# Linear attention and an affine MLP on one core: one k-v layout for batches 2 to 7, the bias column in batch 1, g on VectorE, and a re-planned order

## The chip, the cores and the metric

The kernel runs on one core of one Trainium2 chip, in one launch. The core has five engines that matter here: TensorE (PE in the profile), VectorE (DVE), ScalarE (ACT), GpSimd (POOL), and SyncE (SP), which here only issues transfers. Each engine takes its own instructions strictly in order and waits on semaphores for the others. The metric is device time in microseconds, the median of several runs.

## The reference

The inputs are q, k and v of shape [8 batches, 8 heads, 576 rows, 64], and the parameters of a residual MLP with affine scales in place of a norm. All is float32.

```python
kv  = einsum('bhsd,bhse->bhde', k, v)            # 64 x 64 for each head
out = einsum('bhsd,bhde->bhse', q, kv)
x   = out / sqrt(mean(out**2, -1) + 1e-6) * g_norm   # heads side by side: [8, 576, 512]
a1  = alpha1 * x + beta1
tok = einsum('ts,bsd->btd', w_tok, a1)           # w_tok: 576 x 576
u   = x + lam * tok
a2  = alpha2 * u + beta2
out = u + lam * (relu(a2 @ w_ch1) @ w_ch2)       # 512 -> 2048 -> 512
```

## The kernel before

The kernel does not issue instructions as it is read. `Prog.op` records every operation with its engine (or a choice of engines), a cost in microseconds, what it reads and writes, and a priority. `plan` then derives urgencies from a few operations with due times, schedules all operations several times in a model (`schedule`), shuffles a few priorities (`shake`, with the seeds given to `plan`), and keeps the order. The instructions of each engine are emitted in that order, with semaphore waits where a result crosses engines. While the first channel matmul has not started, the model fills TensorE's idle time with warming matmuls on zeros (L1429 in the profile), so the number of these is a planned figure, fixed when the kernel is built.

For each of the eight batches the work is:

1. *Loads.* k, v and q of a batch come by SP. For batch 0, a row of the tile holds nine consecutive tokens of one head (`nine`). For batches 1 to 7 (`load_kv`) it holds four consecutive ones of the first 512 (`kf`, `vf`), and the 64 tokens from 512 on stand in tiles of their own (`kft`, `vft`), by two more loads each.
2. *The k-v product* (float32). Batch 0: `kv_first`, L628, two groups of 36 matmuls that contract over 64 rows. Batches 1 to 7: `kv_groups`, two groups of 16 matmuls over 128 rows (L691) and one of 8 over the 64 rows of the tails (L701). The result is split into a high and a low bfloat16 part (`kvd`) by ScalarE (L718) and VectorE (L723, L726).
3. *The q-kv product and the norm* (`qkv_groups`). q is split the same way (L501, L582) and transposed, for batches 0 and 1 by TensorE, later by transfers. The products are L789 for batch 0 (float32), L782 with L401 for the others, and `tail` (L863) for the last 64 tokens. Then come a square on ScalarE (L819), a sum over each head on VectorE (L821), a square root and a reciprocal, and x without g (L840). Two multiplications follow: by alpha1, lam and g into the bfloat16 operand of the token mix (`rt`, `rtt`; L844, L892), and by g into x itself, on GpSimd (L848, L895).
4. *The token mix* (`tok_groups`, L920 and L942; batch 0: `tok_first`, L972). It contracts over 576 tokens in five passes. The last pass holds the 64 tail tokens and one row with beta1 times lam, against which `wt` has a row with the sums of w_tok's rows. For even batches the tail tokens stand in partitions 0 to 63 and the beta1 row in 64, for odd ones in 64 to 127 and 0, so that `wt` keeps the tail rows and the sums twice (chunks 4 and 5). VectorE adds the result to x (L927).
5. *a2, transposed* (`a2t`). Batches 0 and 1: transposed on TensorE (`ut_pe`, L1007), with alpha2 and beta2 applied as the columns are evacuated (L1016, L1017). Later batches: only alpha2 is applied (L933), and a transfer transposes. Their beta2 enters as a bias of the ReLU (`hb`), beta2 times w_ch1.
6. *The channel matmuls.* `ch1_groups`: 16 tiles of 128 hidden columns (L1056 for even batches; L1075 for odd ones, which take the tail tokens of two batches along). In batch 0, each of its 64 matmuls is followed by one of a single column that multiplies beta2 by the same weights (L401 on `b2c`); these 16 columns become `hb`. Then `ch2_groups` (L1121; L1102 at the very end).

TensorE interleaves the end of one batch with the start of the next: the second channel matmul of a batch hides the token mix's evacuation, the k-v product of the next batch but one and the transpositions.

The weights are loaded on the same SP queue behind the first k, v and q, in the order w_tok, batch 1, w_ch1 in four parts, lam, w_ch2 in four parts. w_ch1 is converted to bfloat16 by ScalarE and VectorE (L501, L502), w_ch2 is multiplied by lam by VectorE and GpSimd (L1357).

Of the kernel before, what the change touches and what calls it, by code (L numbers as in the profile page):

```python
# [15 lines left out]
NH = 8  # L16
S = 576
# [32 lines left out]
class Prog:  # L50
# [6 lines left out]
    def __init__(self, nc, stack):  # L57
# [9 lines left out]
        self.spare = 0.0  # L67

# [54 lines left out]
    def plan(self, due, rounds, seeds):  # L123
# [40 lines left out]
        def shake(pri, seed):  # L164
            rnd = random.Random(seed)
            return {o: pri[o] + (rnd.gauss(0.0, 2.0) if rnd.random() < 0.1 else 0.0)
                    for o in movable}
# [12 lines left out]
    def schedule(self):  # L180
# [67 lines left out]

        while left:
            progressed = False  # L250
            for e, q in queues.items():
                while q and free[e] <= t + 1e-9:
# [3 lines left out]
                    for o in cands:  # L256
# [4 lines left out]
                        if isinstance(o.eng, tuple) and better_elsewhere(o, e, t):  # L261
                            continue
# [144 lines left out]
def bass_transnormer_attn__then__resmlp_affine_kernel(  # L407
# [15 lines left out]
    with ExitStack() as stack:  # L423
# [14 lines left out]
        b2c = sb("b2c", [128, 4], BF16)  # L438
        hb = sb("hb", [128, 16], F32)
        eps = sb("eps", [128, 1], F32)  # L440
        kf = sb("kf", [128, 2, NH, 4, DH], F32)
        vf = sb("vf", [128, 2, NH, 4, DH], F32)
        qf = sb("qf", [128, NH, 4, DH], F32)
        kft = sb("kft", [128, 2, 4, DH], F32)
        vft = sb("vft", [128, 2, 4, DH], F32)
# [18 lines left out]
        a2t = sb("a2t", [128, 4, TP], BF16)  # L464
# [9 lines left out]
        def nine(tile, a):  # L474
            return tile[:, a].rearrange("p h c d -> p (h c d)")[:, 0:1152].rearrange(
                "p (x c d) -> p x c d", x=2, c=9)

# [38 lines left out]

        HALVES = (slice(0, 4), slice(4, 8))
        ALL = (slice(0, 8),)

        def load_first(a):  # L520
            for key, src, tile in (("kf", k, kf), ("vf", v, vf)):
                P.op("SP", 0.6, lambda e, src=src, tile=tile: e.dma_start(
                    nine(tile, a).rearrange("p x c d -> p x (c d)"),
# [11 lines left out]
        def load_kv(b, go=()):  # L535
            j = (b + 1) % 2
            for tile, tl, src, n in ((kf, kft, k, "kf"), (vf, vft, v, "vf")):
                P.op("SP", 0.6, lambda e, tile=tile, src=src: e.dma_start(
                    tile[:, j].rearrange("p h c d -> p h (c d)"),
                    src[b, :, 0:512, :].rearrange("h (p c) d -> p h (c d)", c=4)),  # L540
                    r=go, w=[(n, j)], dma_us=3.4)
                for g in range(2):
                    P.op("SP", 0.5, lambda e, tl=tl, src=src, g=g: e.dma_start(
                        tl[64 * g:64 * g + 64, j],
                        src[b, 4 * g:4 * g + 4, 512:576, :].rearrange("h s d -> s h d")),
                        w=[(n + "t", j, g)], dma_us=0.4)
# [71 lines left out]

        def kv_first():

            def group(a):
                t = P.ptile(2)

                def f(e):
                    for c in range(9):
                        for x, y in ((0, 0), (0, 1), (1, 0), (1, 1)):
                            r = slice(64 * y, 64 * y + 64)
                            m = e.matmul(t.ap(slice(64 * x, 64 * x + 64))[:, y, 0:64],  # L628
# [833 lines left out]
```

## Time and profile before

| | |
|---|---|
| median of 3 runs | 368.38 us (367.87 to 368.93) |
| the profiled execution | 368.05 us, of which the span is 366.2 us |
| TensorE busy | 360.6 us, 98% |
| VectorE busy | 198.4 us, 54% |
| ScalarE busy | 159.2 us, 43% |
| GpSimd busy | 81.7 us, 22% |
| moved | 59.87 MB in 92423 packets, 163 GB/s on the mean |

The lines of the profile read: line of the kernel, engine, operation, output and inputs, shape, count, then busy time, mean duration in ns, and the engine's idle time ahead of it with what ended it. In rows in order of time the first two numbers are the start and the length of a group of alike instructions in microseconds, from the first one's start to the last one's end. A matmul's listed length includes its way through the array and overlaps the next one's, so the distance between starts is what it takes of TensorE's time. A float32 matmul that isn't a transposition appears as two records: "x72" of L628 is 36 matmuls.

### The profile page before, as it was taken

To read this page: it belongs to the slowest core of one execution; us is meant where nothing else is said; L and a number is where in the kernel's file an instruction comes from. 1 tells how busy PE (TensorE), PEld (TensorE's weight loads), DVE (VectorE), ACT (ScalarE), POOL (GpSimd) and SP (SyncE) were. 2 spreads that over 40 slices of the span, in tenths; PEclk is the share of its full clock that TensorE was granted. 3 is DMA by queue.
4 is the path that set the end of the run, shared out by engine and by line. 5 is a ranking of instruction groups with operands and counts; after the bars stand their busy time and mean duration, and the time that the engine had idled before them with its cause. 6 is when DMAs were issued, how large, how long until landed. Compare 5 with 4: busy or idle time off the path is not lost.

```text
span 366.2 us, 7069 instructions
## 1 busy us (share of the span) xinstructions
PE 360.6 (98%) x3164; PEld 205.8 (56%) x2876; DVE 198.4 (54%) x313; ACT 159.2 (43%) x268; POOL 81.7 (22%) x71
## 2 busy tenths in 40 slices
PE   7999999999999999999999999999999999999996
PEld 3787445467754554457654554457654554457644
DVE  4287699773973197735764176915933165720021
ACT  2464974237830298107650188107630186007600
POOL 4064602700450007100530006400620006200000
PEclk9999999999999999999999999999999999999999
DMA  8999999999777897439904499233404110420012
GB/s 257 319 290 319 384 382 273 265 250 249 211 141 158 246 259 178 101 94 309 230 18 115 138 304 177 50 110 85 90 7 108 59 30 0 59 100 30 0 57 88
DMA packets 92423, 59.87 MB, mean 163 GB/s; under 512 B 59549, under 2 KB 82341, under 8 KB 92264
## 3 DMA queue, kind: packets, MB, share of 16 engines
q1 hardware_dynamic: 92368, 59.41, 62.5%
q8 instruction: 24, 0.39, 0.5%
q14 instruction: 7, 0.06, 0.0%
q10 hardware_dynamic: 24, 0.01, 0.0%
HBM read 38.56 MB, written 9.44 MB: 131 GB/s over the span
## 4 chain that ended last, share of the span: by engine, by line
PE 97%; DMA 2%; SPq 0%; DVE 0%; issue 0%
PE ps L1121 34%; PE ps L1075 19%; PE ps L1056 16%; PE ps L920 8%; PE ps L691 4%; DMA qf<-in_q_dram 2%; PE ps L401 2%; PE ps L782 2%; PE ps L789 1%; PE ps L942 1%; PE ps L972 1%; PE ps L1007 1%; PE ps L1429 1%; PE ps L649 1%; PE ps L1102 1%; PE ps L701 1%
## 5 line engine op out<-in xcount | busy, mean ns | idle before, releaser
L1121 PE MATMUL ps<-w,ht 128*128 128x512 bf16 x560 | 126.0, 379 | 0.0
L848 POOL TENSOR_TENSOR xm<-xm,g_bc 128x512 f32<-128x512 f32 (+1 forms) x36 | 47.4, 1316 | 186.6 <-DVE rt L844 184.7
L1121 PEld LDWEIGHTS ps<-w,ht 128*128 128x128 bf16 x560 | 53.1, 98 | 63.0 <-issue 1.2
L1045 ACT ACTIVATE ht<-ps,hb 128x512 bf16<-128x512 f32 (+1 forms) x96 | 70.5, 739 | 40.5 <-PE ps L1075 32.8
L1075 PE MATMUL ps<-a2t,w 128*128 128x320 bf16 x512 | 71.9, 299 | 0.0
L1075 PEld LDWEIGHTS ps<-a2t,w 128*128 128x128 bf16 x512 | 49.3, 98 | 20.2 <-ACT ht L1045 0.3
L1056 PE MATMUL ps<-a2t,w 128*128 128x512 bf16 x256 | 59.7, 379 | 0.0
L1131 DVE TENSOR_TENSOR xm<-ps,xm 128x512 f32<-128x512 f32 x31 | 21.4, 689 | 50.4 <-PE ps L1121 50.3
L718 ACT ACTIVATE kvd<-ps 64x128 bf16<-64x128 f32 x28 | 7.6, 271 | 78.5 <-PE ps L701 78.1
L1056 PEld LDWEIGHTS ps<-a2t,w 128*128 128x128 bf16 x256 | 24.3, 97 | 29.6 <-issue 1.2
L821 DVE TENSOR_REDUCE small<-sq 128x16 f32<-128x1024 f32 (+2 forms) x20 | 20.5, 1028 | 22.9 <-ACT sq L819 22.9
L920 PE MATMUL ps<-rt,wt 128*128 128x512 bf16 x112 | 28.8, 379 | 0.0
L501 ACT ACTIVATE qs<-qf 128x1024 bf16<-128x1024 f32 (+1 forms) x15 | 14.2, 964 | 26.7 <-DMA qf<-in_q_dram 26.1
L927 DVE TENSOR_TENSOR xm<-ps,xm 128x1024 f32<-128x1024 f32 x14 | 17.1, 1222 | 14.5 <-PE ps L920 14.5
L1046 ACT ACTIVATE ht<-ps 128x512 bf16<-128x512 f32 (+1 forms) x32 | 20.6, 650 | 6.8 <-PE ps L1075 3.3
L819 ACT ACTIVATE sq<-ps 128x1024 f32<-128x1024 f32 (+2 forms) x20 | 17.4, 873 | 7.3 <-PE ps L789 4.3
L840 DVE TENSOR_TENSOR xm<-ps,small 128x1024 f32<-128x1024 f32 (+1 forms) x18 | 19.8, 1103 | 0.4
L723 DVE TENSOR_TENSOR kvd<-ps,kvd 64x128 bf16<-64x128 f32 x28 | 8.1, 288 | 20.5 <-ACT kvd L718 20.0
L844 DVE TENSOR_TENSOR rt<-xm,e1g_bc 128x1024 bf16<-128x1024 f32 (+1 forms) x17 | 19.0, 1125 | 0.1
L582 DVE TENSOR_TENSOR qs<-qf,qs 128x1024 bf16<-128x1024 f32 x12 | 15.3, 1284 | 6.8 <-ACT qs L501 6.8
L920 PEld LDWEIGHTS ps<-rt,wt 128*128 128x128 bf16 x112 | 10.9, 98 | 12.9 <-issue 0.4
L691 PEld LDWEIGHTS ps<-vf,kf 128*64 128x64 f32 x448 | 14.2, 138 | 5.0 <-issue 5.0
(119 smaller groups left out, 334.2 us busy)
## 6 DMA issues: line engine op xcount, KB each, us to landing
out_dram<-xm SPq DMA_DIRECT2D x31, 256.0 KB, 2.5
kf<-in_k_dram SPq DMA_DIRECT2D x7, 1024.0 KB, 10.3
vf<-in_v_dram SPq DMA_DIRECT2D x7, 1024.0 KB, 8.0
qf<-in_q_dram SPq DMA_DIRECT2D x7, 1024.0 KB, 8.0
stg<-in_moe_w_ch_dram SPq DMA_DIRECT2D x3, 1024.0 KB, 13.8
kf<-in_moe_w_ch_dram SPq DMA_DIRECT2D x2, 1024.0 KB, 14.6
kf<-in_k_dram SPq DMA_DIRECT2D x2, 576.0 KB, 5.2
vf<-in_v_dram SPq DMA_DIRECT2D x2, 576.0 KB, 6.3
```

Source lines behind the costliest of these rows:

```text
L691: m = e.matmul(out(h), kf[:, buf, h, c, :], vf[:, buf, h, c, :], start=(c == 0 and h < 4 * a + 2), stop=False, skip_group_check=True)
L821: P.op("DVE", dve_us(64 * m), lambda e: e.tensor_reduce(out=smv, in_=sqv.rearrange("p (h d) -> p h d", h=m), axis=AX.X, op=ALU.add), r=[(" ...
L840: P.op("DVE", dve_us(64 * m), lambda e: e.tensor_tensor(out=x3, in0=split(raw()), in1=inv, op=ALU.mult), r=[t, ("sm", sms)], w=xk, pri=-200)
L844: lambda e: e.tensor_tensor(out=r_, in0=x, in1=eb, op=ALU.mult),
L848: P.op("POOL", pool_us(64 * nh), lambda e, xc=xc: e.tensor_tensor(out=xc, in0=xc, in1=g_bc[rows, None, :].to_broadcast([nr, nh, DH]), op=A ...
L920: m = e.matmul(t.ap()[:, i, :], tok_w(b, sc, c), rsrc(b, sc), start=(sc == 0), stop=(sc == 4))
L1045: o = P.op("ACT", act_us(n) + 0.09, lambda e: e.activation(dst, src(), ACT.Relu, bias=hb[:, fj:fj + 1]) if b > 1 else e.activation(dst, sr ...
L1046: dst, src(), ACT.Relu, bias=hb[:, fj:fj + 1]) if b > 1 else e.activation(
L1056: m = e.matmul(t.flat(), w, a2t[:, dj, 0:512], start=(dj == 0), stop=(dj == 3))
L1075: m = e.matmul(t.ap()[:, i, 0:320], w1[:, dj, 128 * fj:128 * fj + 128], a2t[:, dj, 320 * i:320 * i + 320], start=(dj == 0), stop=(dj == 3))
L1121: m = e.matmul(t.flat(), ht[:, fj, 128 * c:128 * c + 128], w2[:, fj, :], start=(fj == 0), stop=(fj == 15))
L1131: P.op("DVE", dve_us(512), lambda e: e.tensor_tensor(out=x, in0=t.flat(), in1=x, op=ALU.add), r=[t] + keys, w=keys)
```

## The change

- k and v of batches 2 to 7 are loaded in batch 0's layout, nine tokens to a row, by one load each. `kv_product` serves batch 0 and, through `kv_nine`, these; the new evacuation does for each of the two groups what was done behind the third. Batch 1 keeps its form, with its tails in the free end of the same tile.
- The beta2 column moves from batch 0 to batch 1: `a2t` gets a column 640 with beta2, and in `odd` the second half of each tile takes 321 columns instead of 320. Sixteen copies of one column (`hb[:, fj]`) replace one of sixteen.
- Batch 0's first four tiles of the first channel matmul are computed in two halves, `front` and `back`, over two of the four contracted chunks each.
- From batch 2 on, VectorE multiplies x by g, over the pair of row blocks at once.
- The tail rows of the mix's operand always stand in partitions 0 to 63 with the beta1 row at 64. The second copy in `wt` and its sums are no longer made. Another form of the mix is added behind `MIX = 8`, which no batch reaches; two operations that only that form needs stay (a copy of `wt`'s tail rows, and beta1 loaded once more and multiplied by lam).
- The planner: a rule `sooner` (ScalarE, VectorE and GpSimd don't start a less urgent operation if a more urgent one becomes ready within half its cost), a different `shake` and seed, costs changed for batch 0's q-kv product and two evacuations, and parameter rows loaded in the order of the list.

The order of the instructions of every engine changes with it. The core of the diff:

```diff
+            share, by = (0.02, 0.1, 0.3)[seed % 3], (1.0, 3.0)[seed % 2]
+            return {o: pri[o] + (rnd.gauss(0.0, by) if rnd.random() < share else 0.0)
...
+        def sooner(o, e, t):
+            cost = o.cost[e] if isinstance(o.cost, dict) else o.cost
+            until = t + self.look * cost
...
+                    if t + 1e-9 < at <= until:
+                        return True
+            return False
...
+                        if e in ("ACT", "DVE", "POOL") and sooner(o, e, t):
+                            continue
...
-        def load_kv(b, go=()):
+        def load_kv(b):
             j = (b + 1) % 2
+                if b > 1:
+                    P.op("SP", 0.6, lambda e, src=src, tile=tile: e.dma_start(
+                        tile[:, j].rearrange("p (z f) -> p z f", z=4),
+                        src[b].rearrange("(z y) (p c) d -> (y p) z (c d)", y=2, c=9)),
+                        w=[(n, j)], dma_us=3.1)
+                    continue
...
+        def kv_product(b, a):
+            j = a if b == 0 else (b + 1) % 2
+            t = P.ptile(2)
+            def f(e):
+                for c in range(9):
+                    for x, y in ((0, 0), (0, 1), (1, 0), (1, 1)):
+                        r = slice(64 * y, 64 * y + 64)
+                        m = e.matmul(t.ap(slice(64 * x, 64 * x + 64))[:, y, 0:64],
+                                     nine(kf, b, a)[r, x, c, :], nine(vf, b, a)[r, x, c, :],
+                                     start=(c == 0), stop=(c == 8), skip_group_check=True)
+                return m
+            P.op("PE", 1.22, f, r=[("kf", j), ("vf", j)], w=[t])
+            return t
...
+        def kv_nine(b):
+            kv5 = kvd[:].rearrange("p (a x y) i d -> p a x y i d", a=2, x=2)
+            def group(a):
+                t = kv_product(b, a)
+                for x in range(2):
...
         def kv_groups(b):
+            if b > 1:
+                yield from kv_nine(b)
+                return
...
-                    P.op("PE", 0.28 * nc_, f32, r=QT + KVD + [("kv32", h0 // 4, i)
+                    P.op("PE", 0.55 * nc_ + 0.02, f32, r=QT + KVD + [("kv32", h0 // 4, i)
...
-                    P.op("POOL", pool_us(64 * nh), lambda e, xc=xc: e.tensor_tensor(
-                        out=xc, in0=xc, in1=g_bc[rows, None, :].to_broadcast([nr, nh, DH]),
+                    P.op("POOL" if b < 2 else "DVE", pool_us(n) if b < 2 else dve_sb(n),
+                         lambda e, xc=xc, gb=gb: e.tensor_tensor(
+                             out=xc, in0=xc, in1=gb, op=ALU.mult),
...
-                        if b == 0:
-                            m = P.matmul_held(hbt.flat()[:, fj:fj + 1], w, b2c[:, dj:dj + 1],
-                                              dj == 0, dj == 3)
...
+            def front(fj):
+                held[fj] = t = P.ptile(1)
+                def f(e):
+                    for dj in range(2):
+                        m = e.matmul(t.flat(), w1[:, dj, 128 * fj:128 * fj + 128],
+                                     a2t[:, dj, 0:512], start=(dj == 0), stop=False)
...
+                            n = 321 if (b, i) == (1, 1) else 320
...
+                if b == 1:
+                    P.op(act_dve(1), 0, lambda e: copy(
+                        e, hb[:, fj:fj + 1], t.ap()[:, 1, 320:321]), r=[t], w=[("hb", fj)])
...
-        spread_load(moe_alpha2, a2_bc, "a2")
+        spread_load(moe_alpha2, a2_bc[:], "a2")
+        spread_load(moe_beta1, stg[:, 0, 0, :], "st0")
         P.chain = False
+        P.op("DVE", dve_sb(512), lambda e: e.tensor_tensor(
+            out=lam_bc[:], in0=stg[:, 0, 0, :], in1=lam_bc[:], op=ALU.mult),
+            r=["st0"], w=["lam", "e2"], port=True)
+        P.op("DVE", 0.4, lambda e: e.tensor_copy(out=wt[64:128, 5, :], in_=wt[0:64, 4, :]),
+             r=[("wtm", 4)], w=["wt5"], port=True)
...
-        P.plan(due, 8, (15,))
+        P.plan(due, 8, (56,))
```

More of the change, by code (lines that the diff above doesn't have):

```diff
@@ L700, in f @@
                         rows = slice(64 * (h // 4), 64 * (h // 4) + 64)
-                        m = e.matmul(out(h), kft[rows, buf, h % 4, :], vft[rows, buf, h % 4, :],
+                        m = e.matmul(out(h), rows64(kf)[rows, h % 4, :], rows64(vf)[rows, h % 4, :],
                                      start=False, stop=True, skip_group_check=True)
                     return m
-                P.op("PE", 0.4, f, r=[(n + "ft", buf, g) for n in "kv" for g in range(2)], w=ts)
+                P.op("PE", 0.4, f, r=[(n + "ft", g) for n in "kv" for g in range(2)], w=ts)
                 for a in range(2):
```

255 lines of the change are left out of this document (166 added, 89 removed).

## The prediction

> **What bounds the kernel now.** I read the page's busy shares and the granted clock first, then the chain of work that ended last, then the order of time on TensorE.
>
> ```profile
> span 366.2 us, 7069 instructions
> PE 360.6 (98%) x3164; PEld 205.8 (56%) x2876; DVE 198.4 (54%) x313; ACT 159.2 (43%) x268; POOL 81.7 (22%) x71
> PEclk9999999999999999999999999999999999999999
> PE 97%; DMA 2%; SPq 0%; DVE 0%; issue 0%
> ```
>
> TensorE is 97% of the chain and its clock is full, so the time is the sum of what stands on TensorE's queue. But not all of that is work: warming matmuls fill planned waits.
>
> ```profile
> L1429 PE MATMUL ps<-a2b 128*128 128x512 bf16 x32 | 9.3, 437 | 1.9 <-DVE a2b L1226 1.9
> ```
>
> So a gain has two sources: real work taken off TensorE, or, in the stage before the first channel matmul, a wait (warming) that gets shorter. Everything on the other engines is free as long as its result is there when TensorE's fixed order reaches it. What a matmul costs is the distance from its start to the next one's, since its listed duration overlaps the next.
>
> **The change, part by part.** The new constant for the mixing form is 8 and the batches are 0 to 7, so its branches never run: the mix stays in five full passes for each of four row blocks.
>
> *The bias column.* Batch 0 loses its 64 one-column matmuls (four behind each of 16 tiles). Their price, in order of time, with the price of the same matmul without them from the chain:
>
> ```profile
> 38.72 0.38 PE L1056 MATMUL ps<-a2t,w 128*128 128x512 bf16 x1
> 38.96 0.38 PE L1056 MATMUL ps<-a2t,w 128*128 128x512 bf16 x1
> 58.61 12.95 PE ps L1121 x60
> L501 ACT ACTIVATE hb<-ps 128x16 f32<-128x16 f32 x1 | 0.2, 178 | 0.0
> ```
>
> A pair takes 0.24 us (38.72 to 38.96), a bare matmul 12.95/60 = 0.216; so 64 x 0.024 = 1.55 us go. In their place batch 1 streams one more column in 64 matmuls of 320 (under 1/320 of each, some 0.03 us in all), and 16 small copies take the column out. At 0.18 us each, by the copy above, they are 2.8 us on ScalarE and VectorE, spread over batch 1's first channel matmul, on neither's path to TensorE. Cover gone, at worst each holds its tile's ReLU 0.2 us longer. I take -1.55.
>
> *The k-v products of batches 2 to 7.* Before: two blocks of full-height matmuls and one for the rows 512 to 575. After: two blocks of 36 half-height matmuls, the form batch 0 already has.
>
> ```profile
> 119.97 1.15 PE L691 MATMUL ps<-vf,kf 128*64 128x64 f32 x32
> 121.06 1.90 PE L1121 MATMUL ps<-w,ht 128*128 128x512 bf16 x8
> 122.89 1.15 PE L691 MATMUL ps<-vf,kf 128*64 128x64 f32 x32
> 125.80 0.46 PE L701 MATMUL ps<-vft,kft 64*64 64x64 f32 x16
> 127.07 0.59 PE L1056 MATMUL ps<-a2t,w 128*128 128x512 bf16 x2
> 6.63 1.28 PE L628 MATMUL ps<-vf,kf 64*64 64x64 f32 x72
> 7.84 0.60 PE L1429 MATMUL ps<-a2b 128*128 128x512 bf16 x2
> ```
>
> From 119.97 to 127.07 are 7.10 us with 20 other matmuls (8, 8 and 4) of 0.216, so one batch's products cost 2.78 us. The eight between 121.06 and 122.89 take 1.83 instead of 1.73: each entry into such a block costs 0.10. The new form's block is 7.84 - 6.63 = 1.21 us; no row shows one entered from the channel matmuls. Without an entry price two blocks cost 2.42 and gain 0.36; with 0.10 at entry, 2.62 and 0.16; with 0.10 at exit too, 2.82 and -0.04. I take the middle, the nearest row being the entry into L691: 6 x 0.16 = -1.0 us, ends -2.2 and +0.2. The Trainium skill, "TensorEngine Tiling (Array Packing)", Key Properties, says that changing the tiling mode drains the engine. By that rule each block pays at both ends and the sum would hold +0.2 here in place of -1.0; the trace agrees at the entries and, at 7.84, shows no such price at the exit.
>
> Moving each product's operands by one load of 2304 byte runs in place of three (the main rows and two tails) only takes transfers and issues off SP's queue. The new beta1 row is loaded ahead of batch 2's k and waits for the conversion of the first quarter of w2, which holds that k and all behind it on SP.
>
> ```profile
> 46.60 0.37 SPq L538 DMA_DIRECT2D kf<-in_k_dram  x1
> 47.09 4.90 DVE L1357 TENSOR_TENSOR w<-stg,lam_bc 128x512 bf16<-128x512 f32 x8
> 78.42 1.15 PE L691 MATMUL ps<-vf,kf 128*64 128x64 f32 x32
> ```
>
> Four of those eight steps end at about 49.5, so k is issued some 3 us later and TensorE wants it at 78.4, 29 us on. Nothing; without that cover it would cost the 3.
>
> *The stage before the first channel matmul.* The planner gets other costs, another rule (a short look ahead before it starts a less urgent operation) and another seed; the order that comes out has 25 warming matmuls instead of 32 and puts the broadcast of alpha1 where TensorE waited for q. The rows, the last one from the chain:
>
> ```profile
> 7.69 0.49 SPq L1222 DMA_DIRECT2D ht<-in_moe_w_tok_dram  x1
> ht<-in_moe_w_tok_dram SPq DMA_DIRECT2D x1, 144.0 KB, 11.6
> 15.33 1.16 PE L789 MATMUL ps<-kvd,qt 128*128 128x128 f32 x8
> 16.42 1.97 PE L649 MATMUL ps<-ident,qf 128*64 128x128 f32 x32
> 18.58 1.68 PE L1429 MATMUL ps<-a2b 128*128 128x512 bf16 x7
> 20.10 1.95 PE L789 MATMUL ps<-kvd,qt 128*128 128x128 f32 x16
> 21.89 0.64 PE L1260 MATMUL ps<-ident,ht 128*128 128x128 f32 x4
> 36.53 2.11 PE L1429 MATMUL ps<-a2b 128*128 128x512 bf16 x9
> 38.47 0.38 PE L1056 MATMUL ps<-a2t,w 128*128 128x512 bf16 x1
> 39.58 0.47 PE ps L605 x8
> ```
>
> w_tok has landed at 7.69 + 11.6 = 19.3, but TensorE first reads it at 21.89. In the new order its first transposition comes ahead of the second half's q-kv products. All else that precedes it is done by 18.58 in the old order, and what the new one swaps there (four warming matmuls in, the wait for q out) cancels within some tenths, so the landing decides and it starts at 19.4. From there to 36.53 the old order has 14.64 us of work; the new one adds those products as two blocks of 1.09 (15.33 to 16.42), five warming matmuls of 0.216 and one block of q transpositions of 0.47: 19.4 + 14.64 + 2.18 + 1.08 + 0.47 = 37.8. Before it was 38.47, and that block lay behind it; the gain is 0.7 + 0.47 = 1.2 us. Ends: 1.6, if the two blocks cost no more than the one of 1.79 did (20.10 to 21.89), and -0.5, if a short step that I haven't priced comes late on VectorE's queue, where the new order leaves about 0.3 us at the tightest place (the second half's rt). The second copy of w_tok's last rows and its row of sums leave ScalarE and VectorE here; one copy that no matmul reads any more, and later a product of beta1 and lam (0.61 each at most, as the eight steps at 47.09), come onto VectorE, the product behind batch 1's rt: nothing. The first four channel tiles split in halves of 2 + 2 matmuls add no work; they only start before the last two transposed columns are evacuated.
>
> What is late next is the first token mix of batch 1. Its operand depends on loads that don't move:
>
> ```profile
> 54.85 2.98 DVE L1357 TENSOR_TENSOR w<-kf,lam_bc 128x512 bf16<-128x512 f32 x3 [0.21 <-DMA kf<-in_moe_w_ch_dram]
> 59.70 1.22 DVE L821 TENSOR_REDUCE small<-sq 128x16 f32<-128x1024 f32 x1 [0.74 <-ACT sq L819]
> 67.02 1.23 DVE L844 TENSOR_TENSOR rt<-xm,e1g_bc 128x1024 bf16<-128x1024 f32 x1
> 71.40 0.81 PE L920 MATMUL ps<-rt,wt 128*128 128x512 bf16 x3
> ```
>
> VectorE waits for w2's last quarter, then makes rt by 68.25. TensorE comes to the mix at 71.40 now; after, 1.2 + 1.55 us earlier and with four channel matmuls (0.86) moved behind it, at 67.8. The new order does both reductions first, and the old one idled 0.74 between them, so rt is there at about 67.7. I take 0.1 us of new wait; 0.5 if rt stays at 68.25. More gain from the first stage would be given back here.
>
> *g on VectorE.* From batch 2 on the multiplications by g leave GpSimd.
>
> ```profile
> L848 POOL TENSOR_TENSOR xm<-xm,g_bc 128x512 f32<-128x512 f32 x28 | 40.9, 1459 | 184.1 <-DVE rt L844 182.7
> L582 DVE TENSOR_TENSOR qs<-qf,qs 128x1024 bf16<-128x1024 f32 x12 | 15.3, 1284 | 6.8 <-ACT qs L501 6.8
> L892 DVE TENSOR_TENSOR rtt<-xtl,e1g_bc 64x512 bf16<-64x512 f32 x7 | 6.7, 951 | 0.2
> 169.73 1.25 PE L1075 MATMUL ps<-a2t,w 128*128 128x320 bf16 x8
> 180.43 1.21 DVE L844 TENSOR_TENSOR rt<-xm,e1g_bc 128x1024 bf16<-128x1024 f32 x1
> 213.25 1.03 PE L1056 MATMUL ps<-a2t,w 128*128 128x512 bf16 x4
> 226.74 0.81 PE L920 MATMUL ps<-rt,wt 128*128 128x512 bf16 x3
> ```
>
> No row has this step on VectorE; the nearest of its size take 1.21 (at 180.43) to 1.28 (L582), and I take 1.22. Two of these and one of 0.95 (L892) are 3.4 us a batch, on an engine 54% busy. Only the first stands ahead of rt in the new order. In batch 3 rt was there 181.64 - 169.73 = 11.9 us after the first products; with one step of 1.22 in between it is 13.1. In an even batch TensorE leaves 226.74 - 213.25 = 13.5 us between the first products and the mix, and 1.7 more in the new order (eight channel matmuls moved ahead). So 2.1 us are left, and more in an odd batch: nothing. Without that slack it is 1.22 us for each batch.
>
> The sum: -1.55 - 1.0 - 1.2 + 0.1 = -3.65. The profiled execution took 368.05 (its span and 1.85 around it) and becomes 364.4; the median of the runs lies 0.33 above it, so 364.7.
>
> **The rivals.** (a) *The first stage gives nothing*: w_tok's transpositions start earlier, but VectorE's in-order steps or rt of batch 1 hold TensorE as before. For it: rt hangs on the load at 54.85 with almost no room left. Against: the old order shows 19 warming matmuls after the first 13 where the new one needs 12. Then -1.55 - 1.0: 365.8. (b) *The new k-v form pays drains at both ends*: +0.2 in place of -1.0, 365.9; against it stands the row at 7.84. It is what the rule of the Trainium skill cited above would give. (c) *VectorE becomes the bound, slower*: place, the mix of even batches. If the other two g steps and a batch's two large subtractions of q (1.22 + 0.95 + 2 x 1.28 = 4.7) in effect run before rt, the 2.1 us are exceeded by 2.6 in each of batches 2, 4 and 6, 7.9 in all: 372.6. It decides from a delay of about 3.3 us a batch, where the excess outweighs the gain; the order of instructions has none of these ahead of rt, so only lengthened durations could do it, and with GpSimd idle I see no reason for these. (d) *Nothing moves*: gains eaten by waits of planned tightness, within 0.3%: 367.9.
>
> **How the numbers follow.** 0.3% (1.1 us) is about what this measurement can tell from no change. Forecast (363.5 to 365.3) 0.58, (a) 0.17, (b) 0.10, (c) 0.08, (d) 0.07. Forecast, (a) and (b) are faster: 0.85; same 0.07, slower 0.08. The range goes down to 363.4 (k-v at -2.2 with the rest as taken) and up to 367.0, past (a) and (b) and the first stage's worse end.
>
> **What would show it.** Right: no one-column matmuls, 25 warming ones, the first channel matmul near 37.8, the first mix of batch 1 near 67.9 behind at most 0.5 us of wait, batches' k-v products at 2.6 us, and TensorE without waits from then on, GpSimd silent after batch 1. Wrong: waits of TensorE on VectorE in front of the mixes, on ScalarE or VectorE after the second k-v block (where about 1 us is left), or a first channel matmul no earlier than 38.

## The result, and the profile after

The changed kernel takes 366.37 us (median; 365.94 to 366.78), the kernel before, run beside it, 368.23 us (367.66 to 368.93). The ratio is 0.9951 with a 95% interval of 0.9934 to 0.9967: faster by 1.9 us, where 3.65 were forecast. The profiled execution took 365.94 us, its span is 363.8.

The first lines of the profile's page after the change, and its chain of work by engine:

```profile
span 363.8 us, 7681 instructions
PE 356.6 (98%) x3477; PEld 205.2 (56%) x3253; DVE 221.3 (61%) x345; ACT 159.9 (44%) x273; POOL 33.3 (9%) x35
PE 93%; DVE 5%; issue 1%; ACT 0%
```

TensorE still bounds the kernel, but VectorE now has 5% of the chain, where it had 0%. The waits of TensorE in the changed kernel (who waited, for what; us in total, times, longest):

```profile
PE ps L1572 <- DVE a2b L1368: 1.9, 1, 1.9
PE ps L1020 <- DVE xm L1035: 1.7, 1, 1.7
PE ps L1211 <- DVE hb L534: 0.3, 1, 0.3
```

The first is the start of the program and was there before. The other two are new. TensorE in order of time, in the changed kernel:

```profile
1.86 5.05 PE L1572 MATMUL ps<-a2b 128*128 128x512 bf16 x13 [1.86 <-DVE a2b L1368]
6.84 1.28 PE L666 MATMUL ps<-vf,kf 64*64 64x64 f32 x72
...
36.66 0.61 PE L644 MATMUL ps<-identb,qs 128*128 128x128 bf16 x8
37.11 0.59 PE L1184 MATMUL ps<-a2t,w 128*128 128x512 bf16 x2
...
67.14 1.03 PE L1020 MATMUL ps<-rt,wt 128*128 128x512 bf16 x4
...
70.61 1.89 PE L1260 MATMUL ps<-w,ht 128*128 128x512 bf16 x8
74.17 1.04 PE L1020 MATMUL ps<-rt,wt 128*128 128x512 bf16 x4 [1.67 <-DVE xm L1035]
...
81.18 3.44 PE L1211 MATMUL ps<-a2t,w 128*128 128x320 bf16 x24
...
103.22 1.03 PE L1020 MATMUL ps<-rt,wt 128*128 128x512 bf16 x4
...
120.58 1.28 PE L666 MATMUL ps<-vf,kf 64*64 64x64 f32 x72
121.79 1.90 PE L1260 MATMUL ps<-w,ht 128*128 128x512 bf16 x8
123.62 1.28 PE L666 MATMUL ps<-vf,kf 64*64 64x64 f32 x72
124.83 1.04 PE L1260 MATMUL ps<-w,ht 128*128 128x512 bf16 x4
125.70 1.89 PE L1169 MATMUL ps<-a2t,w 128*128 128x512 bf16 x8
```

What answers to these rows in the kernel before, beside those that the prediction shows:

```profile
1.86 4.48 PE L1429 MATMUL ps<-a2b 128*128 128x512 bf16 x13 [1.86 <-DVE a2b L1226]
6.27 0.43 PE L1198 MATMUL ps<-xtl,ones 1*128 1x64 f32 x2
...
82.87 1.40 PE L1075 MATMUL ps<-a2t,w 128*128 128x320 bf16 x9
...
103.47 1.03 PE L920 MATMUL ps<-rt,wt 128*128 128x512 bf16 x4
```

Set side by side they give the ledger below. Work that only changed its place (one block of q transpositions of 0.45 us, two groups of four channel matmuls of 0.86 each) is counted where it stood before.

| stretch of TensorE's time | forecast | measured, us |
|---|---|---|
| the first 13 warming matmuls (4.41 to 4.98) | 0 | +0.57 |
| from their end to the first channel matmul (32.20 to 30.27, less 0.45) | -1.2 | -2.38 |
| to the first mix of batch 1 (32.93 to 30.03, plus 1.31) | -1.55, and +0.1 of wait | -1.59 |
| to the first channel matmul of batch 1 (11.47 to 14.04, less 0.86) | one of six k-v gains, -0.16 | +1.71 |
| to the mix of batch 2 (20.60 to 22.04, less 0.86) | 0 | +0.58 |
| from there to the end (262.73 to 260.58, plus 0.86) | five of six k-v gains, -0.8 | -1.3 |

The sum is -2.4, the difference of the two spans. I take the first row for chance: this stretch is the same 13 matmuls in both kernels, and over the profiles of this study its row is between 4.30 and 5.73 us long. That is as wide as the spread of the runs of one kernel (367.66 to 368.93). The later runs are therefore also compared from the start of the first k-v product (6.84 here) to the end of the span: **356.96 us** for the changed kernel. Counted from the end of the warming stretch, the kernel before takes 366.2 - 6.27 = 359.93, so in these two executions the work behind the start got 3.0 us shorter, where the medians differ by 1.9. That the medians hold unequal starts is argued from the two rows, not shown for each run.

So the change gained more than forecast in the first stage, and gave it back in batch 1. VectorE and GpSimd around the long wait, in the changed kernel:

```profile
65.48 0.68 DVE L1532 TENSOR_TENSOR lam_bc<-stg,lam_bc 128x512 f32<-128x512 f32 x1
66.08 4.50 DVE L621 TENSOR_TENSOR qs<-qf,qs 128x1024 bf16<-128x1024 f32 x2
70.51 1.75 DVE L621 TENSOR_TENSOR qs<-qft,qs 64x512 bf16<-64x512 f32 x1
72.29 0.69 DVE L1270 TENSOR_TENSOR xm<-ps,xm 128x512 f32<-128x512 f32 x1
72.90 1.21 DVE L1035 TENSOR_TENSOR xm<-ps,xm 128x1024 f32<-128x1024 f32 x1
```

```profile
65.64 3.87 POOL L936 TENSOR_TENSOR xm<-xm,g_bc 128x512 f32<-128x512 f32 x2 [1.86 <-DVE rt L915]
69.58 2.13 POOL L995 TENSOR_TENSOR xtl<-xtl,g_bc 64x512 f32<-64x512 f32 x1
```

The second half of batch 1's mix needs the PSUM banks that the mix addition L1035 empties. In VectorE's queue there now stand ahead of that addition the product of beta1 and lam that nobody reads, all three subtractions of batch 2's q, and an output addition of batch 0. TensorE had written the addition's input by 70.8 us (its last matmul starts at 70.39 and is 0.38 long); VectorE came to it at 72.90. Two of these subtractions take 4.50 us beside GpSimd's multiplications by g. In the kernel before, one of them took 1.22 with GpSimd idle (its multiplications had ended at 72.08):

```profile
72.21 1.22 DVE L582 TENSOR_TENSOR qs<-qf,qs 128x1024 bf16<-128x1024 f32 x1
```

Three causes offer themselves: the order, the length, and the dead product (the one of beta1 and lam). The experiments separate them.

### The profile page after: what moved, and what is told of

Its sections match the earlier page's. It is cut to its first block, busy times and chain, and to the rows that moved or that the text cites. A ratio compares the mean times of both kernels' runs of the same rounds, so it can differ in the third digit from the quotient of the medians.

```text
span 363.8 us, 7681 instructions
## 1 busy us (share of the span) xinstructions
PE 356.6 (98%) x3477; PEld 205.2 (56%) x3253; DVE 221.3 (61%) x345; ACT 159.9 (44%) x273; POOL 33.3 (9%) x35
## 4 chain that ended last, share of the span: by engine, by line
PE 93%; DVE 5%; issue 1%; ACT 0%
PE ps L1260 30%; PE ps L1211 19%; PE ps L1169 14%; PE ps L1020 8%; PE ps L666 5%; PE ps L1572 2%; PE ps L428 2%; PE ps L851 2%; PE ps L858 1%; PE ps L1083 1%; DVE qs L621 1%; PE ps L1118 1%; PE ps L693 1%; PE ps L1053 1%; DVE xm L909 1%; PE ps L1241 1%
## 5 line engine op out<-in xcount | busy, mean ns | idle before, releaser
L1158 ACT ACTIVATE ht<-ps,hb 128x512 bf16<-128x512 f32 (+1 forms) x96 | 70.8, 739 | 42.9 <-PE ps L1211 33.2
L1211 PE MATMUL ps<-a2t,w 128*128 128x320 bf16 (+1 forms) x512 | 72.2, 299 | 0.3 <-DVE hb L534 0.3
L1211 PEld LDWEIGHTS ps<-a2t,w 128*128 128x128 bf16 x512 | 49.3, 98 | 20.9 <-DVE xm L909 0.7
L1169 PE MATMUL ps<-a2t,w 128*128 128x512 bf16 x240 | 54.9, 379 | 0.0
L728 ACT ACTIVATE kvd<-ps 64x128 bf16<-64x128 f32 x24 | 6.5, 271 | 86.5 <-PE ps L666 86.4
L1169 PEld LDWEIGHTS ps<-a2t,w 128*128 128x128 bf16 x240 | 22.5, 98 | 25.0
L1035 DVE TENSOR_TENSOR xm<-ps,xm 128x1024 f32<-128x1024 f32 x14 | 17.1, 1220 | 11.4 <-PE ps L1020 11.3
L666 PEld LDWEIGHTS ps<-vf,kf 64*64 64x64 f32 x1008 | 16.0, 135 | 5.4 <-issue 5.3
L733 DVE TENSOR_TENSOR kvd<-ps,kvd 64x128 bf16<-64x128 f32 x24 | 6.9, 288 | 18.6 <-ACT kvd L728 18.4
L666 PE MATMUL ps<-vf,kf 64*64 64x64 f32 x1008 | 17.9, 221 | 0.0
L621 DVE TENSOR_TENSOR qs<-qf,qs 128x1024 bf16<-128x1024 f32 x12 | 16.6, 1395 | 0.0
## 6 DMA issues: line engine op xcount, KB each, us to landing
kf<-in_moe_w_ch_dram SPq DMA_DIRECT2D x2, 1024.0 KB, 12.4
```

Of the source, the lines that this page charges most:

```text
L621: lambda e, hi=hi, lo=lo, src=src: e.tensor_tensor(out=lo, in0=src, in1=hi, op=ALU.subtract), r=kin + kh, w=kl, port=True)
L666: m = e.matmul(t.ap(slice(64 * x, 64 * x + 64))[:, y, 0:64], nine(kf, b, a)[r, x, c, :], nine(vf, b, a)[r, x, c, :], start=(c == 0), stop= ...
L1158: o = P.op("ACT", act_us(n) + 0.09, lambda e: e.activation(dst, src(), ACT.Relu, bias=hb[:, fj:fj + 1]) if b > 1 else e.activation(dst, sr ...
L1169: m = e.matmul(t.flat(), w, a2t[:, dj, 0:512], start=(dj == 0), stop=(dj == 3))
L1211: m = e.matmul(t.ap()[:, i, 0:n], w1[:, dj, 128 * fj:128 * fj + 128], a2t[:, dj, 320 * i:320 * i + n], start=(dj == 0), stop=(dj == 3))
```

## The experiments

All but one start from the changed kernel. The order is edited after planning: `names[...]` are operations of the plan, and `move` puts some directly behind another. Times "from the first k-v product" are as defined above.

**The order, first attempt.**

```diff
+    move(P, [names["out", 0, 0]], names["mix", 1, 0])
+    # sub4: names["sub", 2, 4, 0]; late: its transposing transfer;
+    # last: the last evacuation of batch 2's k-v products on VectorE
+    move(P, [sub4] + late, last)
```

> Against the changed kernel, VectorE makes batch 1's first mix addition before the subtraction of batch 2's q tails and before batch 0's first output addition; the tails' subtraction (and the transfer that transposes it) goes behind the evacuation of batch 2's k-v products. All work is kept. Theory 'order': the 1.67 us wait of TensorE in the middle of batch 1's mix comes from what stands ahead of that addition, so the addition starts when the matmuls are done (70.8), the second half of the mix starts at about 72.4 instead of 74.17, the first channel matmul of batch 1 at about 79.7 instead of 81.18, and the time falls by 1.2 to 1.7 us (median about 365.0). Rival 'VectorE is full': between 57 and 78 us VectorE has no gap, so the wait only moves to the transpositions of u; the channel matmul stays within 0.4 us of 81.18 and the time within 0.4 of 366.4.

Median 367.51 us (365.77 to 370.12), ratio 0.9982 (0.9954 to 1.001). Five of the ten runs take at most 366.69 us and five 368.33 or more; the profiled one is of the longer ones (369.47). From the first k-v product it takes 359.78, 2.8 more than the changed kernel. TensorE in order of time, and SyncE's transfers:

```profile
73.06 1.03 PE L1047 MATMUL ps<-rt,wt 128*128 128x512 bf16 x4
...
93.53 0.64 PE L978 MATMUL ps<-kvd,qt 128*64 128x64 bf16 x16 [3.28 <-DMA qt<-qs]
94.10 2.32 PE L1238 MATMUL ps<-a2t,w 128*128 128x320 bf16 x8
```

```profile
82.64 6.54 SPq L655 DMA_TRANSPOSE qt<-qs  x1
```

The wait in the mix is gone, so the place in the order is needed for it. But the transfer, now behind the loads of batch 3's k and v, was late by 3.28 us. And the eight matmuls behind that pause take 2.3 us where eight took 1.25 (the row at 90.10 in the changed kernel is 1.26 long): with 1.8 us gained at the mix, 3.28 and some 1.2 lost here give the 2.8.

**The order, mended.**

```diff
+    move(P, [names["out", 0, 0]], names["mix", 1, 0])
+    move(P, [sub4], names["mix", 1, 2])
+    # its transposing transfer: ahead of the load of batch 3's q on SP
```

> The order alone, mended: the tails' subtraction of batch 2's q goes directly behind batch 1's second mix addition, its transposing transfer ahead of the load of batch 3's q (in the first attempt it stood behind the loads of batch 3's k and v, landed late and cost TensorE 3.28 us), and batch 0's first output addition behind the first mix addition. The dead product stays. Theory 'order': the wait in the middle of the mix is gone, the transfer is in time, and the time falls by 1.0 to 1.7 us against the changed kernel (ratio to before about 0.991). Rival 'VectorE is full': the subtraction of 0.7 us in front of the evacuations of u puts back 0.6 us or more, and the ratio stays at 0.994 or above.

Median 364.27 us (363.46 to 364.85), ratio 0.9878 (0.9856 to 0.99); from the first k-v product 355.18, a gain of 1.8 on the changed kernel. TensorE's only wait behind its start:

```profile
PE ps L1241 <- DVE hb L561: 0.3, 1, 0.3
```

All of the wait went and nothing came in its place. With the same work on VectorE, the order alone suffices; VectorE being full from 57 to 78 us doesn't bind.

**The length: GpSimd taken away.**

```diff
-                        out=xc, in0=xc, in1=gb, op=ALU.mult),
+                        out=xc[:, 0:1, 0:1], in0=xc[:, 0:1, 0:1],
+                        in1=g_bc[rows, None, 0:1], op=ALU.mult),   # batch 1 alone
```

> Against the changed kernel, batch 1's multiplications by g on GpSimd are done on one column instead of 512 (batch 1's output lacks g in the sum x + lam * tok, which is the part left out); order and everything else stay. Theory 'contention': GpSimd's work beside VectorE is what lengthens the two subtractions of batch 2's q from 2 x 1.28 to 4.50 us and the tails' one from 0.7 to 1.75; without it they take 2.6 and 0.7, the mix addition starts at 70.8, the wait of 1.67 us falls to 0.3 or less, and the time by about 1.6 us (median about 364.8). Rival: the subtractions are as slow by themselves (their operands or their place), the pair stays above 4 us and the wait above 1.3.

Median 363.91 us (363.73 to 364.47), ratio 0.9881 (0.986 to 0.9903); from the first k-v product 355.07, a gain of 1.9. The same steps of VectorE:

```profile
65.58 2.35 DVE L642 TENSOR_TENSOR qs<-qf,qs 128x1024 bf16<-128x1024 f32 x2
67.86 0.67 DVE L642 TENSOR_TENSOR qs<-qft,qs 64x512 bf16<-64x512 f32 x1
```

In the same order the pair takes 2.35 instead of 4.50 us, the third 0.67 instead of 1.75, and the wait is gone. Two causes, then, each of which is needed for the wait: the subtractions stand ahead, and GpSimd lengthens them.

**The dead product.**

```diff
+    P.sequence.remove(names["bl"])     # L1532, lam_bc = beta1 * lam
```

> Against the changed kernel, the product of beta1 and lam that no operation reads is left out; its load stays. Theory: VectorE is late at the mix addition of batch 1 by the sum of what stands ahead, so this step's 0.68 us comes off the wait one for one: 1.0 us of wait instead of 1.67, and a time lower by 0.6 us (median about 365.8). Rival: the steps behind it start earlier but run beside GpSimd for longer or wait for q, so that less than 0.2 us comes off.

Median 364.05 us (363.61 to 364.98), ratio 0.9883 (0.9862 to 0.9905); from the first k-v product 355.27, a gain of 1.7, not 0.6. Why more than its 0.68 us is in the rows of VectorE and GpSimd:

```profile
66.28 3.43 DVE L644 TENSOR_TENSOR qs<-qf,qs 128x1024 bf16<-128x1024 f32 x2
```

```profile
66.44 4.39 POOL L960 TENSOR_TENSOR xm<-xm,g_bc 128x512 f32<-128x512 f32 x2 [1.87 <-DVE rt L938]
```

The first subtraction now starts 0.16 us ahead of GpSimd's step instead of 0.44 behind it, and the pair takes 3.43 instead of 4.50. GpSimd's two take 4.39 instead of 3.87. That the first of the pair ran undisturbed is inferred: 3.43 is one at 1.2 and one at 2.2. My expectation had treated the length of the steps behind as fixed. TensorE's wait in the mix is gone here too, so the dead product is a third cause without which there is none: any one of the three, taken away, suffices.

**The sixteen copies of the bias column.**

```diff
+    for fj in range(16): names["hb", fj].eng = "ACT"
```

> Against the changed kernel, all sixteen copies of the bias column are made by ScalarE instead of half of them by VectorE. Theory: TensorE's 0.34 us wait in batch 1's channel matmul and the 0.2 us beside it come from tiles whose ReLU waits for a copy that stands behind a long step on VectorE; on ScalarE the copy stands directly ahead of its ReLU and costs it 0.2 us at most. The wait goes and the time falls by 0.3 to 0.6 us (median about 365.9). Rival: ScalarE is then the late one, since its queue there also holds the squares of batch 2 (1.02 us each); a wait of the same size stays on ScalarE and the time within 0.2 us.

Median 365.61 us (365.07 to 366.39), ratio 0.9924 (0.9901 to 0.9947); from the first k-v product 356.67, a gain of 0.3. The wait on `hb` is gone from the list; the one of 1.7 us in the mix stays. Of the 0.58 us lost in batch 1's channel matmul the copies' place on VectorE explains half. The rest stands in the same 24 matmuls (here 3.58 us from 87.00 to 90.58, where the 24 from 80.76 on take 3.28); its cause stays open.

**g back on GpSimd from batch 2 on.**

```diff
+    for k, o in names.items():
+        if k[0] == "g" and k[1] > 1: o.eng = "POOL"   # two steps for a pair
```

> One part of the change undone: from batch 2 on the multiplications by g are made by GpSimd again, at the places they have in the order, in two steps of 128 x 512 for each pair. Theory: moving g to VectorE cost and gained nothing, since there is slack on both sides; the time is within 0.4 us of the changed kernel's 366.4. Rival 'g on GpSimd slows VectorE': as in batch 1, VectorE's two-input steps that meet it are lengthened (a subtraction from 1.2 to 2.2 us), TensorE waits before mixes or products of batches 2 to 7, and the time grows by 1 us or more.

Median 366.05 us (365.7 to 366.41), ratio 0.9927 (0.9906 to 0.9949); from the first k-v product 356.91, the changed kernel's within 0.05. This part of the change bought and cost nothing. GpSimd's multiplications meet VectorE's steps in these batches too (from 100 to 330 us the subtractions of 128 x 1024 take 1.29 us on the mean instead of 1.22), but not where TensorE waits: its waits are the same three as in the changed kernel.

**Room in front of the mixes of even batches.**

```diff
+    for b in (2, 4, 6):
+        # names["rt", b, 2] three times more, directly behind it: 3.7 us of VectorE
```

> The changed kernel with the second multiplication that makes rt repeated three times more in batches 2, 4 and 6, so that VectorE is 3 x 1.23 = 3.7 us later with the last part of rt in each even batch. By the slack of 2.1 us that the prediction named, TensorE waits 1.6 us before the mix of each, 4.8 in all. By the changed kernel's trace (in batch 2 the last step of rt ends at 99.09, the mix reads it last from 106.45 on, and starts at 103.22) there is more room: no wait, or at most 0.5 us in all.

One execution: 371.0 us; from the first k-v product 361.42, 4.5 more. The total is close to what the small slack would have given, but the place is another. TensorE, ScalarE and VectorE in order of time:

```profile
106.07 1.85 PE L1052 MATMUL ps<-rt,wt 128*128 128x512 bf16 x4 [2.17 <-ACT ht L1191]
107.71 0.63 PE L1052 MATMUL ps<-rtt,wt 128*128 128x512 bf16 x1
108.14 1.73 PE L1052 MATMUL ps<-rt,wt 128*128 128x512 bf16 x4
...
189.07 1.03 PE L1052 MATMUL ps<-rt,wt 128*128 128x512 bf16 x4
```

```profile
105.31 0.70 ACT L1191 ACTIVATE ht<-ps 128x640 bf16<-128x640 f32 x1 [3.74 <-DVE hb L562]
```

```profile
97.77 5.00 DVE L946 TENSOR_TENSOR rt<-xm,e1g_bc 128x1024 bf16<-128x1024 f32 x4
...
105.12 0.16 DVE L562 COPY hb<-ps 128x1 f32<-128x1 f32 x1
```

The mixes of batches 4 and 6 are not delayed at all (batch 4's starts 4.0 us later behind the first k-v product than in the changed kernel, and so does batch 3's), so their slack is over 3.7 us; the prediction's 2.1 was too small. What stands still is batch 1's channel matmul, beside which batch 2's `rt` is made: a copy of the bias column waits behind the long steps on VectorE, its ReLU on ScalarE waits 3.74 us for it, and TensorE 2.17 us for the tile. Behind the pause the granted clock falls, as this view by stretches shows (busy time, then granted clock, DMA share and GB/s):

```profile
106.00:108.00 2.00, 1.93 (x5) 0.54 0.44 102
108.00:110.00 2.00, 2.00 (x7) 0.61 0.18 38
```

Nine matmuls from 106.07 to 109.71 take 3.64 us instead of 1.94: the pause of 2.17 costs 1.70 more, together 3.9 of the 4.5 us. Most of the rest stands in batch 4's first channel matmul, behind its mix (8 matmuls and 32 short ones take 3.17 us from 212.42 on, 2.66 in the changed kernel); its cause stays open.

**The bias column alone, in the kernel before.**

```diff
-                        if b == 0:
+                        if b == 0 and dj == 0:
                             m = P.matmul_held(hbt.flat()[:, fj:fj + 1], w, b2c[:, dj:dj + 1],
-                                              dj == 0, dj == 3)
+                                              True, True)
```

> The kernel before with 16 of the 64 one-column matmuls of the bias (one behind each tile instead of four; the bias then holds a quarter of its sum, which is the part left out). One part of the change alone: 48 x 0.024 = 1.17 us less on TensorE by the prediction's price, all of it kept, since VectorE has 3 us to spare in front of batch 1's mix here. Expected 1.2 us below before (ratio 0.997). Rival: the columns run beside other matmuls or the gain is waited away before the mix, and the time is within 0.4 us of before.

Median 367.74 us (366.56 to 367.86), ratio 0.9983 (0.9972 to 0.9993). TensorE from the first channel matmul to batch 1's mix:

```profile
38.15 0.38 PE L1056 MATMUL ps<-a2t,w 128*128 128x512 bf16 x1
...
69.89 1.03 PE L920 MATMUL ps<-rt,wt 128*128 128x512 bf16 x4
```

These are 31.74 us where it was 32.93: 1.19 less, against 1.17 by the price of 0.024 us a column. From this mix to the end both take 294.8 us, so nothing of it is waited away. The medians (367.74 against 368.11 beside it) show only 0.4 of it; I put that down to the spread that the start gives them, which is not shown.

**The price of the half-height form.**

```diff
+    # f: a k-v block of nine steps of four matmuls; g: the four channel matmuls behind it
+    kv.fn = lambda e, f=f, g=g: (f(e, 0, 4), g(e, 0, 3), f(e, 4, 9))[-1]
+    n.fn = lambda e, g=g: g(e, 3, 4)
```

> The changed kernel with ten of the twelve k-v blocks of batches 2 to 7 cut in two (16 and 20 of their 36 matmuls) by three channel matmuls that stood behind them; no matmul is added, but ten more entries into the half-height form and ten more exits. Entry alone costs (0.10 us, as the rows of before and after show): 1.0 us more than the changed kernel. The Trainium skill, TensorEngine Tiling (Array Packing), Key Properties, says a change of tiling mode drains the engine; if both ends paid 0.10 the sum would be 2.0 us. If neither end costs, within 0.2 us. The trace shows each block's price directly.

Median 368.81 us (368.01 to 369.31), ratio 1.0014 (1.0004 to 1.0025); from the first k-v product 359.56, 2.6 more than the changed kernel: 0.26 us for each of the ten cuts. One batch:

```profile
121.28 0.69 PE L705 MATMUL ps<-vf,kf 64*64 64x64 f32 x32
121.91 0.82 PE L1300 MATMUL ps<-w,ht 128*128 128x512 bf16 x3
122.66 0.81 PE L705 MATMUL ps<-vf,kf 64*64 64x64 f32 x40
123.40 1.25 PE L1300 MATMUL ps<-w,ht 128*128 128x512 bf16 x5
```

The three channel matmuls between take 0.75 instead of 0.65: 0.10 ahead of the entry. The two parts take 0.63 and 0.74, together 1.37, where the whole block takes 121.79 - 120.58 = 1.21: another 0.16 for each block, inside its own stretch. An entry and an exit together cost 0.26 us, then; whether the 0.16 falls at the block's start or at its end, the rows don't show. The Trainium skill, TensorEngine Tiling (Array Packing), Key Properties, says that a change of tiling mode drains the engine, without a size; the trace agrees in that a change there and back costs time. A rival is that the price comes with the type, since these blocks are float32 between bfloat16. The changed kernel's own trace speaks against it for the entry:

```profile
68.00 0.38 PE L1020 MATMUL ps<-rtt,wt 128*128 128x512 bf16 x1
68.31 1.05 PE L1053 MATMUL ps<-rt,wt 128*64 128x512 bf16 x8
```

Here bfloat16 stands on both sides, only the form changes from 128*128 to 128*64, and the matmul ahead takes 0.31 us instead of 0.22. And the five bfloat16 warming matmuls ahead of float32 transpositions in the form 128*128 (34.71 to 35.79) take 1.08 us, 0.216 each, with nothing on top.

**The warming matmuls.**

```diff
+    # gone: the warming matmuls behind the first thirteen
+    P.sequence = [o for o in P.sequence if o not in gone]
```

> The changed kernel without the twelve warming matmuls behind the first thirteen (three, four and five, at 11.6, 18.3 and 34.7 us). They stand where the plan expected TensorE to wait. Theory: the waits are real, so TensorE stands still instead of warming, the first channel matmul comes at the same distance behind the first k-v product as before (30.27 us) within 0.4 us, and the time is the same within 0.5 us. Rival 1: the plan's costs are too long and the warming matmuls are work in the way: the distance shrinks by up to 12 x 0.216 = 2.6 us. Rival 2: the pauses lower the granted clock and the time grows.

Median 364.28 us (363.89 to 364.6), ratio 0.9879 (0.9861 to 0.9897); from the first k-v product 355.36, a gain of 1.6. TensorE's waits:

```profile
PE ps L1053 <- DVE xm L1068: 1.7, 1, 1.7
PE ps L1435 <- DMA ht<-in_moe_w_tok_dram: 0.6, 1, 0.6
```

Of 12 x 0.216 = 2.6 us only 0.6 was a real wait (for w_tok, whose first matmul starts at 18.23 here) and 0.4 went elsewhere; 1.6 us were work in the way. The granted clock stayed at 1.00 in this stage. The wait in batch 1's mix keeps its 1.7 us although TensorE comes there 1.6 sooner, so VectorE's steps ahead of it follow the kernel's own work and not a load at a fixed time.

**Three causes taken away, then the warming matmuls too.**

```diff
+    move(P, [names["out", 0, 0]], names["mix", 1, 0])
+    P.sequence.remove(names["bl"])                        # the dead product
+    for fj in range(16): names["hb", fj].eng = "ACT"
```

> Three of the causes taken away together: no dead product, all sixteen bias copies on ScalarE, batch 0's first output addition behind batch 1's first mix addition; the subtractions stay where they are. Theory: what the dead product and the copies gave by themselves adds up, as they touch different waits (1.8 us in the mix of batch 1, 0.3 to 0.6 in its channel matmul): TensorE has no wait from batch 1's mix on, the time is 2.1 to 2.6 us below the changed kernel's, about 363.9 and a ratio to before of 0.988. Rival: the two overlap, because whatever comes earlier at the mix waits again in the channel matmul, and the time is the dead product's alone, 364.1 or more.

Median 363.59 us (363.0 to 364.31), ratio 0.9862 (0.9841 to 0.9883); from the first k-v product 354.71, a gain of 2.25. The gains add (1.7 and 0.3 by themselves, and the output addition besides); no wait of TensorE is left behind its start. With the warming matmuls taken out as well:

```diff
+    P.sequence = [o for o in P.sequence if o not in gone]
```

> The three causes taken away together and the twelve later warming matmuls left out as well. Theory: the first thirteen warming matmuls take a length that changes from run to run (4.2 to 5.65 us in the profiles so far), so times are compared from the first k-v product to the end: 356.96 us for the changed kernel, 354.71 without the three causes, 355.36 without the warming matmuls. The warming matmuls stand ahead of the first channel matmul and the waits behind it, so the gains of 2.25 and 1.60 add: 353.1 us from the first k-v product, no wait of TensorE behind the first channel matmul, a median of about 362.2 and a ratio to before of 0.983 to 0.984. Rival: with TensorE 1.6 us earlier, loads that do not move (w2's last quarter, in front of rt of batch 1) hold its first mix, and the 1.6 us are waited away there: 354.7 and a ratio of 0.986 as without the three causes alone.

Median 362.72 us (361.59 to 362.93), ratio to the kernel before **0.984** (0.9826 to 0.9853); from the first k-v product 359.4 - 6.24 = 353.16, where 353.1 was expected. It beats both kernels. Behind its start TensorE waits only for w_tok, 0.6 us.

## Why the prediction was right, and where it was wrong

The sign and the wide range (363.4 to 367.0) held, and TensorE's serial time was the right thing to add up. But the narrow range of the forecast itself, 363.5 to 365.3 with a chance of 0.58, did not hold: 366.37 lies 1.7 us above the forecast of 364.7 and nearer to rivals (a) and (b). Of the terms two were far off, in opposite directions: the first stage gained twice what I took, and batch 1 lost 2.3 us that I had priced at 0.1. That the total stayed within the wide range is in part luck: without the first stage's extra 1.2 us it would have been about 367.5.

*The bias column, -1.55:* right. Measured -1.59 up to the mix, and 1.19 for three quarters of the columns alone.

*"Cover gone, at worst each holds its tile's ReLU 0.2 us longer":* this step failed. A copy of 0.16 us on VectorE holds its ReLU for as long as what stands ahead of it in VectorE's queue: 0.3 us of TensorE's wait in the changed kernel, 3.74 us of ScalarE's when `rt` was lengthened. I priced the copy by its own duration instead of by its queue.

*The k-v products, -1.0:* the mechanism held, the size was 0.25 us a batch (5.12 us from 120.58 to 125.70 with twelve channel matmuls of 0.216, so 2.53, against 2.78), not 0.16. I had charged the new form with two entries and the old one, by the window I chose, without its first. The sentence that the row at 7.84 shows no price at the exit was wrong as well: the block's 1.21 us, which I took as bare work, already holds 0.16 of fixed price. Rival (b) therefore was right that more than the entry is paid, and charged a part of it twice.

*The first stage, -1.2:* measured -2.4 from the end of the first warming matmuls. Two parts failed. w_tok's landing did not decide: it landed at 17.3 (issued at 7.30, 10.0 us to landing), and TensorE's own queue, with four warming matmuls at its end, reached it at 19.20. That is 12.4 us behind the first warming matmuls, where I had 13.1, and 0.8 of the 1.2 us that I missed. And the two blocks of q-kv products cost 0.89 and 0.94 us, not 1.09 each, which is most of the rest. The reading that warming matmuls "fill planned waits" was right about the plan and wrong about the chip: most of the twelve left are not waits.

*"I take 0.1 us of new wait":* the failed step that cost most. I looked only in front of batch 1's first mix; there `rt` was ready (at 65.55, not at my 67.7) and no wait came. The wait of 1.67 us stood inside the same mix, at the addition that empties its first banks. I had followed what the mix reads, not what it writes into, and I had called the dead product nothing because no one waits for it, although it stands in a queue ahead of someone who is waited for.

*g on VectorE, nothing:* right; undone, it changes 0.05 us. The slack was over 3.7 us in batches 4 and 6 rather than 2.1, as shown above.

Rival (a) is refuted in its place, the first stage gave the largest gain; but its mechanism, VectorE's in-order steps that hold TensorE, is what took part of the gain back inside batch 1's mix. Rival (c) named the right engine and the right form (VectorE's lengthened steps at a mix) in the wrong batch: I saw no reason for lengthened steps "with GpSimd idle", and in batch 1 it isn't idle.

## What to carry to other kernels

When a step is moved ahead on a queue, look at every waiter behind it, through the buffers that it empties as well as the data that it makes; a dead or tiny instruction there costs the whole queue's delay. Filler that covers planned waits should be left out once and measured, since the plan's costs may be too long. Where a random stretch at the start is as wide as the effect, count from its end.

## What the runs showed of the hardware that was not expected

- VectorE's subtraction of two operands in SBUF (128 x 1024) takes 1.2 us alone (2.35 for the pair) and about 2.25 beside GpSimd's multiplication; GpSimd's step of 128 x 512 goes from 1.31 (2.62 for two at 61.95 in the run without the dead product) to 1.9 to 2.2. The Trainium skill, GPSIMD Engine Reference, Specifications, says that the two share SBUF interfaces and contend when VectorE has two SBUF inputs; the trace agrees, and a mix addition that reads PSUM kept its 1.22 us beside GpSimd (71.53 in the first attempt at the order). The lengths fit two engines that take turns: in the changed kernel 1.31, 1.2, 1.31 and 1.2 us end to end from GpSimd's start at 65.64 come to 70.66, and the pair of subtractions ended at 70.58. That they take turns is inferred from the sum, not seen.
- The first thirteen warming matmuls take 4.30 to 5.73 us with nothing changed ahead of them. The Trainium skill, TensorE: Matmul & The Clock Gate, Part 1, says that the clock is released by a free-running window, so that the number of slow matmuls varies from run to run; the spread of these rows agrees.
- Behind a pause of 2.17 us the granted clock was 0.54 in the next stretch, behind one of 3.28 us it was 0.50 (94 to 96 us in the first attempt at the order); behind one of 1.67 us it stayed at 1.00 (four mix matmuls in 1.04 us). The two falls were seen in one trace each. In the first attempt the five shorter runs have a mean granted clock of 0.998 to 1.0 and the five longer ones of 0.991 to 0.995, so the fall probably doesn't come every time. The Trainium skill, TensorE: Matmul & The Clock Gate, Part 1, puts the fall at an idle window of about 3.4 us; here a shorter pause sufficed.
